# Down product of the last 1024 tokens with channels on partitions, by seven 2x2 products; weights kept, norm turned

## The chip, the cores and the metric

One core of a Trainium2 chip runs the program. The metric is the time of one execution on the device in microseconds (us), the median of several runs. Besides it there is one profiled execution, whose trace names every instruction of the five engines: PE (matmuls, and PEld for its weight loads), DVE, ACT, POOL, and SP, which here issues the transfers.

## The reference, cut to what matters

```python
mod = (silu(c) @ w_mod).reshape(1, 6, 1, -1)
sa, ca, ga, sb, cb, gb = (mod[:, i] for i in range(6))
h = layernorm(x) * (1 + ca) + sa
x = x + ga * A(h, k, v, ...)            # short and long causal convolution, gated
h = layernorm(x) * (1 + cb) + sb
x = x + gb * ((silu(h @ w_gate) * (h @ w_up)) @ w_down)
```
There are 2048 tokens of 512 channels; the hidden layer has 1792 channels. All is float32. The change concerns the last two lines.

## The kernel before, in words

The first part of the program (convolution through transforms) is not touched. After it the tokens lie in four tiles `xt[0]` to `xt[3]`, each with 128 tokens on the partitions, 4 rows and 512 channels. Tiles 0 and 1 are the first 1024 tokens (`q == 0`), tiles 2 and 3 the second 1024 (`q == 1`).

The feed-forward part goes over blocks `n` from 2 to 27 (`for n in range(G, 2 * NF)`, blocks 0 and 1 are done ahead of it): `f = n % 14` is a block of 128 hidden channels, `q = n // 14` the half of the tokens. So block 14 is the first of the second half and block 27 the last.

**Gate and up** of a block (`gate_up`) are one 2x2 product of matrices of blocks: gate and up against two halves of the 512 channels, and these against two sets of 512 tokens (`t` 0 and 1). It is done by seven products instead of eight (a Strassen-Winograd scheme). The operands of the weights are A11, A12, A22 (tile `wa`) and the sums S1 to S4 (tile `wsum`, made in `sr`); those of the tokens are B11, B21, B22 and the sums T1 to T4 (tiles `op` and `spare`, from the normed tokens `hraw`). Every operand is split into a high half (a cast on ACT to fp32r) and a low half (a subtraction on DVE or POOL); `seventh` is two channel blocks times the three passes of `PASSES`, six matmuls of 128x512. The seven products go into four PSUM tiles: `a` takes numbers 1 and 2, `b` 5 and 3, `c` 7 and 4, `d` 6. `p1` and `p5` are ACT's copies of a and b; DVE adds c to p5 and d to p1, and from these come gate and up for each t, SiLU on ACT, the product on DVE, and high and low halves of the activations `acts`. What belongs to t = 0 is finished in the next block (`late`, `finish`).

**Down** (`down`) is done for groups of G = 2 blocks, 256 hidden channels: for each t and each of 4 rows, six matmuls with the activations as the stationary operand and the down weights (`WD`, tile `wd`, multiplied by gb) moving; DVE adds the result `dn` to `xt`. Eight such products per group are handed out as fillers between the seven products (`downs`), four per block: one behind product 7, one behind 3, two behind 6. The last eight stand alone at the end, each followed by its store.

**Order.** Every instruction is kept in the order in which the program's text issues it on its engine (`InOrder`). Within a block the functions `behind(k)` run what the table `AT` and the loop put behind product k: splitting of the next block's weights (`split_w`, POOL and ACT), their loads, the norm of the second half, and the seven-product operands of the second half. PSUM has eight banks of 512; a tile gets a bank again once its reader is done.

**The norm of the second half**: `norm_stats`, then `norm2b` (tokens times rstd plus shift, on ACT and DVE), then `half_t` (transposes on PE, scale and bias on ACT into `hraw`), in blocks 4 to 8.

Of the kernel before, what the change touches and what calls it, by code (L numbers as in the profile page):

```python
# [10 lines left out]
F32 = mybir.dt.float32  # L11
F32R = mybir.dt.float32r
# [4 lines left out]
P = 128  # L17
# [38 lines left out]
def adaln_h3_swiglu(ctx, tc, q, kT, vT, shk, ssm, dskip, wgu, wdn, c, wmod, e_fwd, e_inv, w_c, out):  # L56
# [9 lines left out]
    def b16(name, shape=(P, 32, P), dt=F32):  # L66
# [3 lines left out]
        "401235670135260172635162432634623634642623634642652376243652376243"  # L70
    )

    def e8(shape, dt, name):
        return wp.tile(shape, dt, tag=f"e8_{next(homes8)}", name=name, bufs=1)
# [447 lines left out]
    def half_t(t, h):  # L522

        n, dst = nrm[t, h], raw_h[0][:, t % 2]
        pts = [p_.rearrange("p (b x) -> p b x", b=2) for p_ in two("nt")]
        for b in range(NB):
            for k in range(2):
                pe.transpose(pts[b // 2][:, b % 2, k * P : (k + 1) * P], n[:, k, b * P : (b + 1) * P], ident)
        for b in range(NB):
            act.activation(  # L530
                dst[:, b, 2 * h * P : 2 * h * P + 2 * P], pts[b // 2][:, b % 2], AF.Identity,
                scale=modT[:, 1, b : b + 1], bias=modT[:, 0, b : b + 1],
            )

# [43 lines left out]
    def split_w(f):  # L585
# [11 lines left out]
        s = e8([P, 2, 4, 2, P], F32R, "wsum")  # L597
# [6 lines left out]
        o = AOP[f] = {n: w[:, :, i] for i, n in enumerate(("A11", "A12", "A22"))}  # L604
        o.update({n: s[:, :, i] for i, n in enumerate(("S1", "S2", "S3", "S4"))})
# [14 lines left out]
    def wd_hi(g):  # L620
        wt = WD[g] = e8([P, 2, G, D], F32R, "wd")
        act.copy(wt[:, 0], stage["d", g])
# [5 lines left out]
    def split_wd(g):  # L628
        wd_mul(g)
        wd_hi(g)  # L630
        wd_lo(g)

# [34 lines left out]
    def downs(n):  # L667
        for _ in range(min(n, len(todo))):
            down(*todo.pop(0))

# [36 lines left out]
    def finish():  # L707

        if late:
            h, c_ = late.pop()  # L710
            act.copy(h[:, 0], c_)
            dve.tensor_tensor(h[:, 1], c_, h[:, 0].bitcast(F32), op=ALU.subtract)

    def gate_up(q, f, at={}):
# [5 lines left out]

        a = one("a")
# [3 lines left out]
        behind(1)  # L725
        b = one("b")
# [4 lines left out]
        behind(5)  # L731
        c_ = one("c")
# [3 lines left out]
        downs(1)  # L736
        seventh(a, f, 2, True)
        sg1 = g2("sg1")
        act.activation(sg1, a, AF.Silu)
        behind(2)  # L740
        seventh(b, f, 3, True)
        behind(3)
        downs(1)
        d = one("d")
        seventh(d, f, 6)
        dve.tensor_tensor(p1, p1, d, op=ALU.add)
        sg2 = g2("sg2")
        dve.tensor_tensor(sg2, p1, b, op=ALU.add)
        act.activation(sg2, sg2, AF.Silu)
        dve.tensor_tensor(d, p5, p1, op=ALU.add)  # L750
        behind(6)
        downs(2)
        dve.tensor_tensor(d, sg2, d, op=ALU.mult)
        h2 = acts[q, f, 1] = slots.pop(0)
        act.copy(h2[:, 0], d)
        seventh(c_, f, 4, True)
        dve.tensor_tensor(h2[:, 1], d, h2[:, 0].bitcast(F32), op=ALU.subtract)
        dve.tensor_tensor(c_, p1, c_, op=ALU.add)
        dve.tensor_tensor(c_, sg1, c_, op=ALU.mult)
        h1 = acts[q, f, 0] = slots.pop(0)  # L760
        late.append((h1, c_))
        behind(4)


    csil = cp.tile([P, 4], F32, name="csil")
    csb = cp.tile([P, 4, 32], F32, name="csb")
# [36 lines left out]
    wc = cp.tile([P, 384], F32, name="wc")  # L803
# [576 lines left out]
    def release(n):  # L1380
# [9 lines left out]
        (4, 7): lambda: norm_stats(2, range(0, 2)),  # L1390
        (4, 6): lambda: norm_stats(2, range(2, 4)),
        (5, 7): lambda: norm2b(2, 0),
        (5, 3): lambda: half_t(2, 0),
        (6, 7): lambda: norm2b(2, 1),
        (6, 3): lambda: half_t(2, 1),
        (6, 2): lambda: norm_stats(3, range(0, 2)),
# [91 lines left out]
```

## Time and profile before

| what | us |
|---|---|
| median of 3 runs | 598.99 |
| the runs | 598.84, 598.99, 601.92 |
| the profiled execution, first to last instruction (span) | 598.0 |
| PE busy | 583.2 |
| DVE busy | 457.0 |
| POOL busy | 329.9 |
| ACT busy | 302.7 |

The profiled execution's own time is given by its span; the runs' median is 1.0 above it. In rows of the timeline the columns are start, duration, engine, line, operation, output<-inputs, shapes and count, and in brackets the idle time before with what ended it. In grouped rows there stand total, mean in ns, and idle time before. Nearly every instruction has line 40, the helper that records it, so the tiles' names tell them apart.

### The profile page before, as it was taken

Reading aid. Unit: us, or ns where it says so; the run is one execution under the profiler, and the core shown is the slowest. Engines: PE = TensorE matmul, PEld = TensorE weight load, DVE = VectorE, ACT = ScalarE, POOL = GpSimd, SP = SyncE. Lnnn points to the kernel's source line nnn. Section 1 sums busy time; section 2 is a strip of 40 time slices with the busy share of each in tenths; the row PEclk is TensorE's granted clock in tenths of the full one; section 3 lists DMA queues with packets and bytes.
Section 4 is the critical chain, followed back from the end, with each engine's and each line's share of the span. In section 5 each row is a group of like instructions: output and inputs, shape, how many; then the busy total and the mean of one; then the engine's idle time right before and its main releaser. Section 6 shows DMA issues by size and latency. Waiting matters only on the chain.

```text
span 598.0 us, 10148 instructions
## 1 busy us (share of the span) xinstructions
PE 583.2 (98%) x4132; PEld 455.0 (76%) x4132; DVE 457.0 (76%) x585; ACT 302.7 (51%) x443; POOL 329.9 (55%) x264
## 2 busy tenths in 40 slices
PE   5999999999999999999999999999999999999997
PEld 4955756535988888888888888788888888888875
DVE  6999989978968878787778868975656565656555
ACT  1897989953574454445544435443434343434320
POOL 0003269692395896757467765766747474747200
PEclk7999999999999999999999999999999999999999
DMA  8998999999011021212120201243212110210003
GB/s 289 412 392 308 227 340 299 210 332 172 33 41 65 21 92 35 71 36 71 36 71 35 71 36 36 71 144 103 71 36 70 36 70 37 70 36 0 1 1 140
DMA packets 35423, 69.00 MB, mean 115 GB/s; under 512 B 2481, under 2 KB 18993, under 8 KB 33074
## 3 DMA queue, kind: packets, MB, share of 16 engines
q1 hardware_dynamic: 35378, 68.37, 37.0%
q8 instruction: 32, 0.52, 0.4%
q14 instruction: 13, 0.11, 0.1%
HBM read 55.78 MB, written 12.58 MB: 114 GB/s over the span
## 4 chain that ended last, share of the span: by engine, by line
PE 85%; DMA 6%; ACT 3%; DVE 2%; SPq 2%; issue 2%; ACTq 0%; DVEq 0%
PE dn L40 25%; PE a L40 12%; PE b L40 11%; PE c L40 11%; PE d L40 6%; PE s L40 5%; PE g L40 3%; DMA X<-away 2%; PE iv L40 2%; PE y L40 2%; PE px L40 2%; PE pk L40 2%; SPq L40 2%; DMA away<-X 2%; PE kt L40 1%
## 5 line engine op out<-in xcount | busy, mean ns | idle before, releaser
L40 PE MATMUL dn<-wd,acts 128*128 128x512 f32 x672 | 166.4, 391 | 0.5 <-DVE acts L40 0.4
L40 PEld LDWEIGHTS dn<-wd,acts 128*128 128x128 f32 x672 | 125.7, 188 | 27.6 <-DVE acts L40 1.1
L40 POOL TENSOR_TENSOR wa<-ws,wa 128x512 fp32r<-128x512 f32 (+1 forms) x52 | 61.7, 1209 | 111.8 <-ACT wa L40 104.0
L40 DVE TENSOR_TENSOR x<-x,dn 128x512 f32<-128x512 f32 x112 | 74.9, 681 | 50.6 <-PE dn L40 49.4
L40 PE MATMUL b<-op,wsum 128*128 128x512 f32 x312 | 79.2, 389 | 0.0
L40 POOL TENSOR_TENSOR wsum<-sr,wsum 128x1024 fp32r<-128x1024 f32 x26 | 71.4, 2745 | 0.0
L40 PEld LDWEIGHTS b<-op,wsum 128*128 128x128 f32 x312 | 58.5, 188 | 12.2
L40 ACT ACTIVATE sg<-sg 128x512 f32<-128x512 f32 x26 | 16.5, 633 | 85.4 <-DVE sg L40 85.4
L40 PE MATMUL a<-op,wa 128*128 128x512 f32 x228 | 57.9, 389 | 0.0
L40 PEld LDWEIGHTS a<-op,wa 128*128 128x128 f32 x228 | 42.8, 188 | 8.9
L40 DVE STREAM_TRANSPOSE X<-X 128x1024 f32<-128x1024 f32 x20 | 46.2, 2338 | 1.1 <-ACT X L40 1.1
L40 ACT CAST acts<-d 128x512 fp32r<-128x512 f32 x26 | 15.3, 587 | 62.5 <-DVE d L40 38.1
L40 POOL TENSOR_TENSOR vt<-u,vt 128x512 f32<-128x512 f32 x8 | 10.1, 1303 | 64.9 <-DMA x<-in_q 50.8
L40 POOL TENSOR_TENSOR s<-s,bcs 128x1024 f32<-128x1024 f32 x16 | 38.8, 2449 | 9.5 <-ACT s L40 9.3
L40 POOL TENSOR_TENSOR sr<-ws 128x256 f32<-128x256 f32 x52 | 43.5, 837 | 0.0
L40 POOL TENSOR_TENSOR wd<-wds,wd 128x1024 fp32r<-128x1024 f32 x14 | 35.4, 2529 | 9.6 <-ACT wd L40 9.6
L40 PE MATMUL c<-op,wa 128*128 128x512 f32 x156 | 39.7, 390 | 0.0
L40 PE MATMUL d<-op,wsum 128*128 128x512 f32 x156 | 39.6, 389 | 0.0
L40 PE MATMUL c<-op,wsum 128*128 128x512 f32 x156 | 39.6, 389 | 0.0
L40 DVE TENSOR_TENSOR acts<-c,acts 128x512 fp32r<-128x512 f32 x26 | 18.0, 692 | 21.5 <-ACT acts L40 21.5
L40 PEld LDWEIGHTS c<-op,wa 128*128 128x128 f32 x156 | 29.2, 188 | 6.3 <-DVE op L40 0.3
L40 PEld LDWEIGHTS d<-op,wsum 128*128 128x128 f32 x156 | 29.3, 188 | 6.1
(109 smaller groups left out, 1089.0 us busy)
## 6 DMA issues: line engine op xcount, KB each, us to landing
ws<-in_wgu SPq DMA_DIRECT2D x28, 512.0 KB, 3.2
wds<-in_wdn SPq DMA_DIRECT2D x14, 512.0 KB, 3.3
wm<-in_wmod SPq DMA_DIRECT2D x6, 1024.0 KB, 13.7
away<-X SPq DMA_DIRECT2D x3, 2048.0 KB, 10.4
X<-away SPq DMA_DIRECT2D x12, 512.0 KB, 11.2
x<-in_q SPq DMA_DIRECT2D x4, 1024.0 KB, 12.8
out<-x SPq DMA_DIRECT2D x16, 256.0 KB, 2.1
kt<-in_kT SPq DMA_DIRECT2D x3, 1024.0 KB, 7.1
```

Source lines behind the costliest of these rows:

```text
L40: return lambda *a, **k: self.tc.keep_in_program_order(f(*a, **k))
```

## The change

1. **Down products of groups 0 to 5 of the second half** are seven products of 2x2 blocks: two blocks of hidden channels and two halves of the output channels, against two sets of 512 tokens. Channels now lie on the partitions of the result. `sum_wd` makes the weights' sums (POOL), `pairs_wd` their high and low halves (`wda`, `wdt`). The activations' seven operands are made by `first_of` (B11, T1, behind block f even) and `second_of` (T2, T3, B22, then B21 and T4). `part_down` is one product for 128 output channels: three matmuls into a tile `dq`. Products 2, 3 and 4 are added to the residual `XT2` at once, products 1, 5, 7 and 6 to accumulators `acc`, which `fold` adds up and into XT2 in blocks 26 and 27. Group 6 is done plainly by `down_t`, weights stationary, with stores into a second output of channels by tokens.
2. **Fillers** in the second half: ten parts in an even block, four in an odd one behind product 1 (`PARTS`); in blocks 14 and 15 the plain down products of the first half. In the second half the order of the products in a block is 1, 5, 7, 6, 3, 2, 4 where it was 1, 5, 7, 2, 3, 6, 4.
3. **The norm** of the second half: mean and deviation go through memory and come back spread over all partitions (`spread`), the tokens are transposed raw (`turn`, kept as XT2), multiplied on POOL and added to on DVE (`times_rs`, `plus_rs`), then scaled on ACT.
4. **Prepared gate and up weights** of blocks 2 to 13 are written to memory in the first half (`keep_w`) and read back in the second (`fetch_w`), where before they were loaded and prepared again.

The first place is PE in block 14. Before, its rows from a's first product to c's second; d<-op,wsum is product 6, a<-op,wa product 2, c<-op,wa product 4 (A22 with T4):

```order
L40 MATMUL a<-spare,wa 128x512 x6
L40 MATMUL b<-op,wsum 128x512 x6
L40 MATMUL c<-op,wsum 128x512 x6
L40 MATMUL dn<-wd,acts 128x512 x6
L40 MATMUL a<-op,wa 128x512 x6
L40 MATMUL b<-op,wsum 128x512 x6
L40 MATMUL dn<-wd,acts 128x512 x6
L40 MATMUL d<-op,wsum 128x512 x6
L40 MATMUL dn<-wd,acts 128x512 x12
L40 MATMUL c<-op,wa 128x512 x6
```
The same block in the changed kernel:

```order
L40 MATMUL a<-spare,wa 128x512 x6
L40 MATMUL b<-op,wsum 128x512 x6
L40 MATMUL c<-op,wsum 128x512 x6
L40 MATMUL dn<-wd,acts 128x512 x6
L40 MATMUL d<-op,wsum 128x512 x6
L40 MATMUL dn<-wd,acts 128x512 x12
L40 MATMUL b<-op,wsum 128x512 x6
L40 MATMUL dn<-wd,acts 128x512 x6
L40 MATMUL a<-op,wa 128x512 x6
L40 MATMUL c<-op,wa 128x512 x6
```
a's second product moved from fifth to ninth place, directly ahead of c's second.

The second place is ACT in the same block, where op<-hraw is the high half of T4 and sg<-a the SiLU of a's second product. Before:

```order
L40 CAST wa<-ws 128x256
L40 CAST wsum<-sr 128x1024
L40 ACTIVATE sg_3748<-a 128x512
L40 CAST op<-hraw 128x1024
L40 ACTIVATE sg_3777<-sg_3777 128x512
L40 CAST acts<-d 128x512
```
And now:

```order
L40 CAST wsum<-sr 128x1024
L40 ACTIVATE b_3832<-b_3832 128x512
L40 ACTIVATE sg_3788<-a 128x512
L40 CAST op<-hraw 128x1024
L40 COPY p_3868<-a 128x512
```
The cast of T4 kept its place behind the SiLU of a, and the other SiLU (of t = 1) moved ahead of both.

The third place is DVE in block 27, from c's sum for p5 to the last low half. Before:

```order
L40 TENSOR_TENSOR p_5206<-p_5206,c 128x512
L40 TENSOR_TENSOR x_542<-x_542,dn 128x512 x2
L40 TENSOR_TENSOR p_5197<-p_5197,d 128x512
L40 TENSOR_TENSOR sg_5256<-p_5197,b 128x512
L40 TENSOR_TENSOR d<-p_5206,p_5197 128x512
L40 TENSOR_TENSOR x_542<-x_542,dn 128x512 x2
L40 TENSOR_TENSOR d<-sg_5256,d 128x512
L40 TENSOR_TENSOR acts<-d,acts 128x512
```
And now, where xt is XT2, and the rows of 1024 with acc are the folds:

```order
L40 TENSOR_TENSOR xt_2623<-xt_2623,acc 128x1024
L40 TENSOR_TENSOR xt_2909<-xt_2909,dq 128x512 x2
L40 TENSOR_TENSOR xt_2909<-xt_2909,acc 128x1024 x2
L40 TENSOR_TENSOR xt_2623<-xt_2623,dq 128x512 x4
L40 TENSOR_TENSOR acts_3860<-c,acts_3860 128x512
L40 TENSOR_TENSOR wds<-wds,bcs 128x1024
L40 TENSOR_TENSOR p_5326<-p_5326,c 128x512
L40 TENSOR_TENSOR p_5294<-p_5294,d 128x512
L40 TENSOR_TENSOR sg_5360<-p_5294,b 128x512
L40 TENSOR_TENSOR d<-p_5326,p_5294 128x512
L40 TENSOR_TENSOR d<-sg_5360,d 128x512
L40 TENSOR_TENSOR acts_3860<-d,acts_3860 128x512
```
Ahead of p5's sum there now stand three folds, six adds of parts, and the multiply of the last group's down weights.

The diff, cut to its core:

```diff
+    def spread(t):
+        w = dp.tile([2, TB, P], F32, tag=f"rs{t}", name=f"rs{t}")
+        sp.dma_start(w.rearrange("k i p -> p k i"), to[f"b{t}"])
+        RS[t] = r4([P, 2, 512], F32, f"rs{t}")
+        sp.dma_start(RS[t], w.rearrange("k i p -> k (i p)")[None].to_broadcast([P, 2, 512]))
...
+    def keep_w(f):
+        w, s = WS[f]
...
+            sp.dma_start(m, t.bitcast(F32))
...
+    def sum_wd(g):
+        st = stage["d", g]
+        pool.tensor_tensor(st, st, bcs[:, None, 2, :].to_broadcast([P, G, D]), op=ALU.mult)
+        a11, a21, a12, a22 = (st[:, k, h * H : h * H + H] for k in range(2) for h in range(2))
+        t = r4([P, 4, H], F32, "wdr")
...
+    ORDER = (1, 5, 7, 6, 3, 2, 4)
+    def part_down(g, n, k):
+        o = one("dq")
+        a, b = ROP[g][PROD[n][0]], LOP[g][PROD[n][1]]
+        for i, (wa, xa) in enumerate(PASSES):
+            pe.matmul(o, a[:, wa, k * P : (k + 1) * P], b[:, xa], start=(i == 0), stop=(i == 2))
+        if n in INTO:
+            t, b0 = INTO[n]
+            xv = XT2[2 + t][:, b0 + k]
+            dve.tensor_tensor(xv, xv, o, op=ALU.add)
+            return
...
+        if g:
+            dve.tensor_tensor(ACC[n][:, k], ACC[n][:, k], o, op=ALU.add)
+        else:
+            act.copy(ACC[n][:, k], o)
...
+    def fold(k):
+        c11, c21, c12, c22 = (XT2[2 + t][:, h : h + 2] for t in range(2) for h in (0, 2))
+        for e, o, i in (
+            ((dve, c11, ACC[1]), (pool, ACC[6], ACC[1])),
+            ((dve, c12, ACC[5]), (dve, c22, ACC[5]), (pool, ACC[7], ACC[6])),
+            ((pool, c12, ACC[6]), (pool, c21, ACC[7])),
+            ((pool, c22, ACC[7]),),
+        )[k]:
+            e.tensor_tensor(o, o, i, op=ALU.add)
...
+    def second_of(f, t, raw):
+        o = LOP[f // G]
+        if t:
+            t3, t2 = RAW["B12"], RAW["T1"]
+            dve.tensor_tensor(t3, raw, t3, op=ALU.subtract)
+            dve.tensor_tensor(t2, raw, t2, op=ALU.subtract)
+            for n, r, e in (("T3", t3, dve), ("T2", t2, pool), ("B22", raw, pool)):
+                o[n] = slots.pop(0)
+                hi_lo(o[n], r, e)
+            return
...
+        def first():
+            seventh(a, f, 2, True)
+            act.activation(sg1, a, AF.Silu)
+            behind(2)
+            fill("a2")
...
+        if q:
+            first()
         seventh(c_, f, 4, True)
...
+    PARTS = ({"c1": 2, "d": 2, "b2": 2, "a2": 2, "c2": 2}, {"a1": 4})
...
+            if m % G == 0:
+                at[3].append(lambda: load_wd(g1))
+                if g1 < NG - 1:
+                    at[6].append(lambda: sum_wd(g1))
+                else:
+                    at[4].append(lambda: fold(0))
+            elif g1 < NG - 1:
+                at[7].append(lambda: pairs_wd(g1))
+            else:
+                at[1].append(lambda: fold(1))
+                at[5].append(lambda: split_wd(g1, 6))
+                at[7].append(lambda: fold(2))
+                at[3].append(lambda: fold(3))
...
-    downs(8)
+    for t in (1, 0):
+        for b in range(NB):
+            down_t(NG - 1, t, b)
```
In the table `AT` the entry `(14, 2): lambda: then("T4", "B21")`, the split of T4, is the same in both kernels.

More of the change, by code (lines that the diff above doesn't have):

```diff
@@ L596, in split_w @@
         pool.tensor_tensor(sr[:, 3], a12, sr[:, 1], op=ALU.subtract)
-        s = e8([P, 2, 4, 2, P], F32R, "wsum")
+        s = e8([P, 2, 4, 2, P], F32R, "wsum", home)
         act.copy(s[:, 0], sr)
@@ new lines, in down_t @@
+    def down_t(g, t, b):
+        o = one("dn")
+        for fl in range(G):
+            for n, (wa, xa) in enumerate(PASSES):
+                pe.matmul(
+                    o, WD[g][:, wa, fl, b * P : (b + 1) * P], acts[1, g * G + fl, t][:, xa],
+                    start=(fl == n == 0), stop=(fl == G - 1 and n == 2),
+                )
+        xv = XT2[2 + t][:, b]
+        dve.tensor_tensor(xv, xv, o, op=ALU.add)
+        sp.dma_start(out_t[b * P : (b + 1) * P, t].rearrange("d i p -> d (i p)"), xv)
```

266 lines of the change are left out of this document (199 added, 67 removed).

## The prediction, made before the changed kernel was run

> **What bounds the kernel now.** I read the page first, then the list of waits of the tensor engine, then a table by stretches, then the timeline of single blocks. The fences stand in this order.
>
> ```profile
> span 598.0 us, 10148 instructions
> PE 583.2 (98%) x4132; PEld 455.0 (76%) x4132; DVE 457.0 (76%) x585; ACT 302.7 (51%) x443; POOL 329.9 (55%) x264
> ```
> ```profile
> PE s L40 <- DMA er<-in_e_fwd: 5.8, 1, 5.8
> PE dn L40 <- DVE acts L40: 0.4, 2, 0.2
> ```
> ```profile
> 387.00:582.00 195.00, 195.00 (x862) 161.50 (x861) 123.76 (x181) 73.35 (x121) 107.89 (x89) 1.00 0.15 53
> ```
> ```profile
> 554.64 1.52 PE L40 MATMUL c<-op,wsum 128*128 128x512 f32 x6
> 556.00 1.52 PE L40 MATMUL dn<-wd,acts 128*128 128x512 f32 x6
> ```
> PE is the bound: from 387 to 582 us it is never idle, at a granted clock of 1.00, and in the whole feed-forward stage it waits 0.4 us, for activations at two places. So what counts there is the number of matmuls times their spacing, plus every wait that the new order lets in. Six matmuls start 1.36 us after the six before them, 0.227 us each; I call this 1.36 us a product. The span is 598.0; the runs' median is 598.99, so about 1.0 lies around the span and I sum against 599.0.
>
> **What is saved.** In six groups the down product takes 7 products of 2 channel blocks of 3 passes, 42 matmuls, where 8 products of 6 took 48. That is 36 matmuls, 36 x 0.227 = 8.2 us off the bound, if PE stays as full as it is. The turned norm leaves PE its 32 transposes, merely bunched; the weights kept in memory cost PE nothing. Everything else is a question of waits, at three places.
>
> **Place one: T4 in block 14.** These rows are the same work in the kernel before: ACT reads a's second product (SiLU), then casts T4's high half, DVE makes its low half, and c's second product needs both.
>
> ```profile
> 377.70 1.53 PE L40 MATMUL a<-op,wa 128*128 128x512 f32 x6
> 378.32 1.22 DVE L40 TENSOR_TENSOR op<-hraw,op 128x1024 fp32r<-128x1024 f32 x1
> 380.71 0.59 ACT L40 ACTIVATE sg<-a 128x512 f32<-128x512 f32 x1
> 382.05 1.05 ACT L40 CAST op<-hraw 128x1024 fp32r<-128x1024 f32 x1 [0.74 <-DVE hraw L40]
> 382.57 2.40 POOL L40 TENSOR_TENSOR wsum<-sr,wsum 128x1024 fp32r<-128x1024 f32 x1
> 383.13 2.92 DVE L40 TENSOR_TENSOR op<-hraw,op 128x1024 fp32r<-128x1024 f32 x1 [0.52 <-ACT op L40]
> 385.87 1.66 PE L40 MATMUL c<-op,wa 128*128 128x512 f32 x6
> 386.10 0.99 PEld L40 LDWEIGHTS c<-op,wa 128*128 128x128 f32 x5 [0.27 <-DVE op L40]
> ```
> Before, five products lay between a's second product (377.70) and c's (385.87), and the low half still came 0.27 late. The change puts a's second product directly ahead of c's, and the split of T4 still hangs behind it, so nothing covers it. From the end of a's product c waits: about 0.2 for the result, SiLU 0.59, cast 1.05, hops 0.1, low half 1.22 when free, less the 0.23 of the one matmul that needs the high half alone: 2.9 us. The dear end: ACT has the other SiLU still to do (0.7 more; its input now waits behind one more add), and the low half takes 2.92 as in the row instead of 1.22: 5.3. POOL's new multiply of the down weights falls into this stretch, but need not hit it; I take 4.4, nearer the row of the same operation.
>
> **What DVE's operations cost.** DVE operations with one operand in PSUM take 0.69 and follow each other by 0.60, or by 0.72 where one needs the other. Those with both inputs in SBUF are another matter:
>
> ```profile
> 428.37 0.69 DVE L40 TENSOR_TENSOR p<-p,d 128x512 f32<-128x512 f32 x1 [0.67 <-PE d L40]
> 429.09 0.69 DVE L40 TENSOR_TENSOR sg<-p,b 128x512 f32<-128x512 f32 x1
> 429.69 1.15 DVE L40 TENSOR_TENSOR d<-p,p 128x512 f32<-128x512 f32 x1
> 444.65 0.69 DVE L40 TENSOR_TENSOR d<-p,p 128x512 f32<-128x512 f32 x1
> ```
> ```profile
> 365.08 2.39 POOL L40 TENSOR_TENSOR wsum<-sr,wsum 128x1024 fp32r<-128x1024 f32 x1
> 370.93 2.40 POOL L40 TENSOR_TENSOR wd<-wds,wd 128x1024 fp32r<-128x1024 f32 x1 [3.46 <-ACT wd L40]
> ```
> ```profile
> 365.15 3.40 DVE L40 TENSOR_TENSOR op<-hraw,op 128x1024 fp32r<-128x1024 f32 x1 [1.29 <-ACT op L40]
> 371.52 2.36 DVE L40 TENSOR_TENSOR d<-p,p 128x512 f32<-128x512 f32 x1
> ```
> ```profile
> L40 DVE TENSOR_TENSOR d<-p,p 128x512 f32<-128x512 f32 x26 | 30.8, 1184 | 0.0
> L40 DVE TENSOR_TENSOR wds<-wds,bcs 128x1024 f32<-128x1024 f32 x13 | 18.4, 1417 | 0.0
> L40 POOL TENSOR_TENSOR wa<-ws,wa 128x512 fp32r<-128x512 f32 x25 | 33.9, 1357 | 105.3 <-ACT wa L40 97.6 <-PE dn L40 7.7
> L40 POOL TENSOR_TENSOR sr<-ws 128x256 f32<-128x256 f32 x50 | 41.1, 822 | 0.0
> L40 ACT COPY p<-a 128x512 f32<-128x512 f32 x26 | 15.3, 590 | 13.1 <-PE a L40 13.1
> ```
> d<-p,p takes 0.69 alone, but 2.36 when it starts 0.6 after a POOL operation of 2.40: it stands until POOL is done (373.33) and then runs. The same holds at 365.15. The mean over 26 is 1.18, so a meeting costs 0.5 on average and up to 2.4. Per pair of blocks the old kernel had two such DVE operations of 512 and one of 1024; the new one has ten of 512 (sums, SiLU times up, T1 to T4, two low halves), while POOL stays about as busy. It was busy 107.89 of 195 us, 55%; now it no longer prepares gate and up weights, but has per pair five low halves of activations (1.36 each), three of down weights (2.4, 1.36 and half of that), the multiply (about 2.4) and four sums (0.82 each): 17.0 of 28.6, 59%.
>
> **Place two: the seam of odd and even blocks.** A pair is now 126 matmuls, 28.6 us, where it was 132, 29.9. DVE has 24 operations with a PSUM operand (24 x 0.62 = 14.9) and ten others (6.9 free, 11.8 at the mean): 21.8 to 26.7 us, so it doesn't bind on average. But behind the odd block they come in a row. From b's second product in the odd block (2.5 us before the even block begins) DVE does gate sum 0.7, five both-SBUF operations, two on c, two more for T4 and B21's low half, p5+c and the add of the first part, 8.2 free, and is done at 5.7. That first part's bank is given to the fifth part, which PE reaches at 9.5. POOL is then at two down-weight low halves (2.4 and 1.36) and two of activations (1.36 each), and meeting all of them costs about 4.2: done at 9.9, 0.4 late. Bounds: 0, if half the meetings miss, and 1.0, if the waits on ACT's casts (0.59 each) add to it. Six even blocks: 0 to 6, taken 2.4.
>
> **Place three: the end.** Here is the end before, in the timeline of PE:
>
> ```profile
> 581.85 1.36 PE L40 MATMUL dn<-wd,acts 128*128 128x512 f32 x4
> 583.43 10.31 PE L40 MATMUL dn<-wd,acts 128*128 128x512 f32 x44 [0.22 <-DVE acts L40]
> ```
> PE waited 0.22 there. Now, in block 27, DVE's queue holds three folds of 1024 and the multiply of the last down weights ahead of p5+c, and the last products need three things at its far end: c's second product needs p5+c, the first down product needs POOL's low half of those weights, its fourth matmul the activations' high and its fifth the low half. DVE, from the seventh part's add in block 26: 16 operations with a PSUM operand (9.9), four of 1024 with both inputs in SBUF (5.3; 1.42 is the mean of the multiply, 1.22 the free one), one of 512 (0.69), one stop for ACT (0.7): 16.6. Counted from the start of block 26, that begins at 13.3 and ends at about 30, where PE as the order has it needs the high half at 29.2: with two small bank waits, 1.2 late. But POOL does two accumulator sums back to back just when the first folds come, and the low half of the weights when d<-p,p comes: 1.2, 1.35 and 1.7 of waiting by the start times this gives, 4.2 in all, so 5.4; and if the seam's backlog (3 us) is still there, 8.4. On the way the bank waits show: d waits for the add of the first part of block 27, which stands behind the folds. I take 6.5. The last store is as before.
>
> By the mean row a meeting is worth 0.5, and the three would come to 1.5 and the end to 2.7 without, 5.7 with the backlog. The Trainium skill ("SBUF — State Buffer", section "Who interferes with whom") says that a DVE instruction with two SBUF inputs fully blocks against a GpSimd operation that reads SBUF until the first is done. By that rule the three cost their whole remainders; the row at 365.15 (1.08 of work behind a wait for 367.47) agrees with the rule, the mean only averages hits and misses.
>
> **What is hidden.** In the first half, blocks 4 to 8, POOL gets four multiplies of 1024 and DVE four adds; POOL stood idle 4.2 us a block ahead of wa's low half (105.3 over 25), and the results are wanted at block 9, so I count nothing; a missed cover would cost up to 1 us. The kept weights:
>
> ```profile
> ws<-in_wgu SPq DMA_DIRECT2D x28, 512.0 KB, 3.2
> away<-X SPq DMA_DIRECT2D x3, 2048.0 KB, 10.4
> ```
> One block's prepared weights are 768 + 1024 KB. By these rows they land in 9 to 11 us; the request waits for c's second product of the block before, and there are at least 13.6 us until use, so nothing again. On SP the two tiny norm transfers stand ahead of a weight load that has a block of slack.
>
> **The sum.** -8.2 + 4.4 + 2.4 + 6.5 = +5.1 on 599.0: 604.
>
> **Rivals.** First, *the saving comes through*: the meetings of DVE and POOL at the seam and the end miss each other. The point that decides is which of the two starts first; at the seam it is 0.35 us between POOL's 1024 low half and DVE's p5+p1. For it: 444.65 ran free, 0.69. Against: the mean of 1.18, and over three times as many tries. Then -8.2 + 2.9 + 0 + 1.2 = -4.1: 595. Second, *half of it*: T4 2.9, seam 0.5, end 4.4: 598.6. Third, *DVE becomes the bound*: each both-SBUF operation meets POOL, the backlog isn't worked off, and each pair loses 1.0: 3.6 more, 608. Against it the 26.7 of 28.6 us. Fourth, *the clock falls* after T4's wait. The rows of the kernel's start, by stretches (the third number from the end is the granted clock):
>
> ```profile
> 5.00:10.00 5.00, 0.13 (x1) 0.00 (x0) 3.94 (x4) 0.20 (x1) 0.00 (x0) 0.86 1.03 381
> 12.00:14.00 2.00, 2.00 (x20) 1.78 (x20) 2.00 (x3) 0.99 (x2) 0.00 (x0) 0.50 1.09 392
> 16.00:18.00 2.00, 1.39 (x14) 1.26 (x11) 2.00 (x5) 0.10 (x1) 0.00 (x0) 1.00 1.08 433
> ```
> After PE's wait of 5.8 us the clock is 0.50 for about 4 us of work: 2 us lost. My wait of 4.4 is shorter and broken by one matmul, so by this row alone it need not fall; if it does, 606. The Trainium skill ("TensorE: Matmul & The Clock Gate", Part 1) puts the idle window that halves the clock at about 3.4 us; by that rule T4's wait would do it, and the trace of before has no wait of this length to say. Fifth, the kept weights land late: at 15 us instead of 11, some 1.4 in each of 12 blocks, 17 more, above 615; the free transfer engines (share 0.15) speak against it.
>
> **How the numbers follow.** Forecast 0.46, own range 600 to 608; saving comes through 0.15; half of it 0.14; DVE bound 0.13; clock 0.08; weights late 0.04. About 0.5%, 3 us, is what a measurement can tell from no change, so "same" is 596 to 602. Faster: 0.12 of the first rival. Same: its other 0.03, 0.14, and 0.08 of the forecast's lower part, 0.25. Slower: 0.38 + 0.13 + 0.08 + 0.04 = 0.63. The range of 8 in 10 leaves out the faster end and the late weights: 596.5 to 609.5.
>
> **What would show it.** In the new profile: 3072 matmuls in the program's order with PE's list of waits holding one of 3 to 5 us on c for op in block 14 (right), or none (place one wrong); PE waits of about 0.4 at dq for an acc add in even blocks; d, c and dn in the last block waiting for DVE and POOL, together 5 to 8. If the dq waits are near 0 and the last block's under 2, the meetings miss and the first rival holds; a time under 596 makes the prediction wrong, as does a wait on the kept weights.

## The result, and the profile after

The changed kernel takes 623.28 us (median of 4 runs, 618.61 to 626.74), the kernel before 600.45 in the runs beside it: a ratio of 1.0375, 95% interval 1.0315 to 1.0435. Slower was forecast, at 604; it is 23 us slower and not 5. The runs of the changed kernel lie 8 us apart, so sizes of a few us are taken from the traces below, between the same instructions of one kernel and the other. A run that fell into a slower state of the chip is left out of medians and ratios here and below; that was one run of e10 (624.16 us).

The page of the changed kernel, span and busy times:

```profile
span 618.9 us, 10224 instructions
PE 586.6 (95%) x4096; PEld 451.4 (73%) x4096; DVE 500.4 (81%) x622; ACT 297.6 (48%) x441; POOL 350.2 (57%) x261
```
PE has 36 matmuls fewer and is no longer full: 95% where it was 98%. From its list of waits (total, times, longest); of these rows the kernel before had only the first:

```profile
PE s L40 <- DMA er<-in_e_fwd: 5.1, 1, 5.1
PE dn L40 <- ACT acts L40: 3.8, 3, 2.6
PE b L40 <- POOL wsum L40: 3.6, 3, 1.9
PE c L40 <- DVE op L40: 2.1, 1, 2.1
PE c L40 <- ACT op L40: 2.1, 1, 2.1
PE a L40 <- ACT p L40: 1.7, 1, 1.7
PE dn L40 <- ACT xt L40: 1.6, 1, 1.6
PE d L40 <- DVE xt L40: 1.5, 1, 1.5
...
PE dn L40 <- POOL wd L40: 1.3, 1, 1.3
PE b L40 <- DVE xt L40: 1.2, 1, 1.2
```
Two of them are place one (c for op), three are place three (d and b for xt, dn for wd). The others, for wsum, for ACT's copies p and xt and most of those for acts, were in no step of the prediction: they lie in blocks 5 to 10, in the first half. PE's first products of block 4 and of block 11 bound that stretch. In the kernel before:

```profile
218.09 1.52 PE L40 MATMUL a<-op,wa 128*128 128x512 f32 x6
326.67 1.52 PE L40 MATMUL a<-op,wa 128*128 128x512 f32 x6
```
And in the changed kernel:

```profile
220.88 1.29 PE L40 MATMUL a<-op,wa 128*128 128x512 f32 x5
344.42 1.52 PE L40 MATMUL a<-op,wa 128*128 128x512 f32 x6
```
108.6 us before, 123.5 now: 15.0 of the 20.9 us between the two spans are lost in blocks 4 to 10, where the down product isn't touched at all. Of the 15.0, PE's waits make 10.5; more than half of the rest is PE at a lower granted clock behind them, 0.92 over block 6 (255.12 to 277.15), where it is busy about 2.5 us longer than in e5 and e8, which have 1.00 there. The rest of the 20.9 by the same reading: the start of the program 2.8 (PE does the same there before and after; in the runs below block 4 begins anywhere between 216.8 and 222.5, so this is scatter), block 14 +4.5, block 15 +1.0, blocks 16 to 26 -5.1, block 27 to the end +2.7.

What stands first in blocks 4 to 7, on SP and on the two engines that split the weights (start, duration, and in brackets the wait ahead):

```profile
231.94 0.37 SPq L40 DMA_DIRECT2D rs<-rsb  x1
243.95 0.32 SPq L40 DMA_DIRECT2D rs<-rs  x1
244.36 0.38 SPq L40 DMA_DIRECT2D ws<-in_wgu  x1
244.80 0.42 SPq L40 DMA_DIRECT2D kept<-wa  x1
...
246.61 0.93 SPq L40 DMA_DIRECT2D ws<-in_wgu  x1
```
```profile
rs<-rsb SPq DMA_DIRECT2D x2, 4.0 KB, 11.2
```
```profile
250.86 0.74 POOL L40 TENSOR_TENSOR sr<-ws 128x256 f32<-128x256 f32 x1 [11.32 <-DMA ws<-in_wgu]
```
```profile
252.64 0.93 ACT L40 CAST wa<-ws 128x512 fp32r<-128x512 f32 x2 [6.18 <-DMA kept<-wa]
```
The norm's store, 4 KB in 1024 pieces of 4 bytes, takes 11 us until it has landed. The load back needs it, so SP stands from 232 to 244, and behind it stand the next weight load, the stores of the kept weights and the weight load after that. POOL then waits 11.32 us for the first, ACT 6.18 us for a kept store that must have read the tile wa before the cast may overwrite it.

### The profile page after: what moved, and what is told of

The parts are those of the page before. It is cut to its first block, busy times and chain, and to the rows that moved or that the text cites. A ratio compares the mean times of both kernels' runs of the same rounds, so it can differ in the third digit from the quotient of the medians.

```text
span 618.9 us, 10224 instructions
## 1 busy us (share of the span) xinstructions
PE 586.6 (95%) x4096; PEld 451.4 (73%) x4096; DVE 500.4 (81%) x622; ACT 297.6 (48%) x441; POOL 350.2 (57%) x261
## 4 chain that ended last, share of the span: by engine, by line
PE 75%; DVE 15%; ACT 4%; DMA 3%; issue 2%; POOL 1%; SPq 0%; DVEq 0%; ACTq 0%; POOLq 0%
PE dn L40 10%; PE b L40 9%; PE a L40 8%; PE c L40 8%; PE dq L40 8%; PE s L40 5%; PE d L40 5%; PE iv L40 4%; PE px L40 3%; PE pk L40 3%; PE g L40 3%; PE y L40 2%; DVE d L40 2%; PE kt L40 2%; DMA wds<-in_wdn 2%
## 5 line engine op out<-in xcount | busy, mean ns | idle before, releaser
L40 PE MATMUL dn<-wd,acts 128*128 128x512 f32 x336 | 84.8, 394 | 4.6 <-ACT acts L40 2.8
L40 PEld LDWEIGHTS dn<-wd,acts 128*128 128x128 f32 x336 | 63.1, 189 | 19.3 <-ACT acts L40 3.7
L40 POOL TENSOR_TENSOR wa<-ws,wa 128x512 fp32r<-128x512 f32 (+1 forms) x28 | 38.4, 1393 | 41.9 <-ACT wa L40 41.9
L40 DVE TENSOR_TENSOR x<-x,dn 128x512 f32<-128x512 f32 x56 | 37.1, 679 | 14.9 <-PE dn L40 14.6
L40 POOL TENSOR_TENSOR s<-s,bcs 128x1024 f32<-128x1024 f32 x16 | 38.8, 2444 | 10.5 <-ACT s L40 10.3
L40 POOL TENSOR_TENSOR acts<-sg,acts 128x512 fp32r<-128x512 f32 x12 | 15.6, 1298 | 41.8 <-ACT acts L40 41.8
L40 PE MATMUL dq<-acts,wdt 128*128 128x512 f32 x144 | 36.9, 391 | 0.0
L40 POOL TENSOR_TENSOR sr<-ws 128x256 f32<-128x256 f32 x28 | 28.4, 1014 | 11.6 <-DMA ws<-in_wgu 11.6
L40 POOL TENSOR_TENSOR wsum<-sr,wsum 128x1024 fp32r<-128x1024 f32 x14 | 34.5, 2464 | 0.5 <-ACT wsum L40 0.5
L40 DVE TENSOR_TENSOR xs<-pk,xs 128x1024 f32<-128x1024 f32 x24 | 28.3, 1217 | 7.1 <-PE pk L40 5.3
L40 PEld LDWEIGHTS c<-op,wsum 128*128 128x128 f32 x156 | 29.2, 188 | 6.5 <-DVE x L40 0.5
```

The lines of the kernel that those rows point to most:

```text
L40: return lambda *a, **k: self.tc.keep_in_program_order(f(*a, **k))
```

## The experiments

Theory one: SP's queue, held by the norm's store. Rival two: the stores of the kept weights by themselves. Rival three: the turned norm's own work and order on POOL, DVE and ACT. All runs in one table; the third column is the stretch of blocks 4 to 10 between the two rows shown above, in each kernel's trace. Each kernel has one trace, of one of its runs.

| run | median us, ratio to before (95%) | blocks 4 to 10 |
|---|---|---|
| before | 599.2 to 601.2 in the six sets of runs beside the others | 108.6 |
| changed | 623.28, 1.0375 (1.0315 to 1.0435) | 123.5 |
| e1 norm behind the load | 619.88, 1.0308 (1.0224 to 1.0392) | 125.1 |
| e2 before, with the norm's trip | 604.45, 1.0068 (1.0033 to 1.0103) | 112.7 |
| e3 before, with kept stores | 599.66, 0.9966 (0.9939 to 0.9993) | 108.7 |
| e4 T4 early | 616.26, 1.0223 (1.0151 to 1.0295) | 123.8 |
| e5 store in rows | 617.22, 1.0278 (1.0231 to 1.0325) | 119.4 |
| e6 before, with trip and kept stores | 613.67, 1.0228 (1.0171 to 1.0284) | 123.7 |
| e7 end folds later | 614.08, 1.0230 (1.0169 to 1.0290) | 122.2 |
| e8 e4, e5 and e7 together | 608.44, 1.0109 (1.0044 to 1.0174) | 117.8 |
| e9 e8 and the norm's order | 598.48, 0.9971 (0.9948 to 0.9994) | 112.6 |
| e10 the norm's order alone | 615.10, 1.0246 (1.0206 to 1.0287) | 122.9 |
| e11 e9 with the 4-byte store | 612.75, 1.0208 (1.0180 to 1.0237) | 124.3 |
| e12 e9, folds between the adds | 598.86, 0.9975 (0.9954 to 0.9995) | 113.7 |
| e13 e9, folds in store order | 599.27, 0.9974 (0.9945 to 1.0003) | 112.5 |
| e14 e9 with T4 late | 605.51, 1.0069 (1.0043 to 1.0094) | 112.4 |
| e15 e9 with the end as changed | 603.44, 1.0037 (1.0009 to 1.0064) | 112.6 |

Kernels that are the same up to block 10 show how far the third column can be trusted: 122.2 to 123.8 (changed, e4, e7), 117.8 and 119.4 (e8, e5), 112.4 to 113.7 (e9, e12 to e15). So it scatters by up to 1.6 us.

### The first half: e1, e2, e3, e6

**e1** moves the two trips behind the weight loads:

```diff
-        (4, 7): lambda: spread(2),
-        (6, 1): lambda: spread(3),
...
             at[7].append(lambda nf=(n + 2) % NF: load_w(nf))
+        if n in (4, 6):
+            at[7].append(lambda t=n // 2 if n == 4 else 3: spread(t))
```


> The changed kernel with one thing moved: the two norm transfers of each tile (spread) stand on SP behind the next gate and up weight load instead of ahead of it, for tile 3 in block 6 after that block's load instead of behind its first product. Theory one (SP's order: the norm store waits for POOL's deviation, its 4 KB take about 11 us to land, SP waits for that before it issues the load back, and the weight load behind it comes 15 us late): of the about 15 us by which blocks 4 to 10 were longer, 10 to 14 go; 609 to 613 us, the tensor engine's waits for wsum under 1 us. Rival two (the stores of the kept weights load the transfer engines and hold buffers) and rival three (the turned norm's own work on POOL, DVE and ACT): nothing of either is touched, 620 to 626 us as the changed kernel, waits as there.

**e2** adds the trip to the kernel before, **e3** adds the kept stores:

```diff
+        RSX[t] = ffn["s"].tile([P, 512], F32, tag="rsx", name=f"rs{t}")
+        sp.dma_start(RSX[t], w.rearrange("k i p -> k (i p)")[0:1].to_broadcast([P, 512]))
...
+        (4, 7): lambda: spread(2),
+        (6, 1): lambda: spread(3),
```
```diff
+        if n < NF:
+            at[2].append(lambda f=f: keep_w(f))
```


> The kernel before, with the norm's trip through memory added at the changed kernel's places on SP (statistics as early as there; the load back brings half as much, 256 KB, and nobody reads it; the norm itself stays the old one). Theory one: the weight loads of blocks 6 and 8 are issued some 12 to 15 us late and PE waits for wsum: 606 to 613 us. Rivals two and three: no kept weights and no new norm work, so 599 to 602 as the kernel before.

> The kernel before, with the prepared weights of blocks 2 to 13 also written to memory (keep_w at the changed kernel's places; nobody reads them back). Rival two: the first half is longer by 8 to 15 us, 608 to 615. Theory one: SP has slack for them and the transfer engines too, at most 2 us: 599 to 603. Rival three: as the kernel before.

Theory one fell in the form in which it was put: in e1 the weight load is no longer behind the store, and the stretch is no shorter, 125.1 where it was 123.5. Kept stores alone cost nothing (108.7), the trip alone 4.1, between what the two theories expected. What e1 has in the load's stead, on SP and ACT:

```profile
229.60 0.37 SPq L40 DMA_DIRECT2D rs<-rsb  x1
240.30 0.32 SPq L40 DMA_DIRECT2D rs<-rs  x1
240.66 0.43 SPq L40 DMA_DIRECT2D kept<-wa  x1
```
```profile
246.61 0.93 ACT L40 CAST wa<-ws 128x512 fp32r<-128x512 f32 x2 [2.47 <-DMA kept<-wa]
257.02 1.05 ACT L40 CAST wd<-wds 128x1024 fp32r<-128x1024 f32 x1 [6.36 <-DMA kept<-wsum]
```
The weights come in time, but their cast waits for the kept store, which now stands behind the norm's store; so does the cast of the down weights, whose tile reuses the place of an earlier wsum. The theory that remained: whatever stands behind the slow store is late, and the kept stores make that a wait on ACT. **e6** puts both into the kernel before, with its old norm and old down product (the edits of e2 and e3 together).

> The kernel before with both additions, the norm's trip through memory (604.5 alone) and the kept weights' stores (599.7 alone); nobody reads either, the old norm and the old down product stay. If the loss is the two together on SP's queue (the kept stores stand behind the norm's store, and hold the buffers of wa and wsum until they have run): clearly more than the sum of the two, 608 to 615. If the two only add: 603 to 605, and the rest of the first half's loss is the turned norm's own work (rival three).

15.1 us, as much as the changed kernel loses there and more than three times 4.1 + 0.1, with none of the turned norm's work. That the two sizes are equal is partly chance, since the changed kernel has a second cause, as e5 shows below. Nor is all of it waiting: PE stands 8.6 us, against 3.3 in e2, and behind the two long waits the granted clock falls, to 0.86 over block 5 (232.87 to 256.79) and 0.84 over block 6 (256.79 to 279.07), where PE is busy 6.3 us longer than before; in e2 the clock stays at 1.00. The waits are the same in kind, first ACT's, then PE's:

```profile
247.48 0.93 ACT L40 CAST wa<-ws 128x512 fp32r<-128x512 f32 x2 [8.10 <-DMA kept<-wa]
...
262.02 1.04 ACT L40 CAST wd<-wds 128x1024 fp32r<-128x1024 f32 x1 [8.73 <-DMA kept<-wsum]
```
```profile
251.51 2.93 PE L40 MATMUL dn<-wd,acts 128*128 128x512 f32 x6 [3.55 <-ACT sg L40]
265.05 1.95 PE L40 MATMUL dn<-wd,acts 128*128 128x512 f32 x3 [3.17 <-ACT acts L40]
```
ACT's queue is in order: behind the waiting cast stand the SiLU and the activations' cast, and PE's down products wait for those, not for weights.

### The store's shape and the norm's order: e5, e10, e9, e11

**e5** turns the 128x8 values on PE and stores 8 rows of 512 bytes; both trips stand between two weight loads:

```diff
-        sp.dma_start(w.rearrange("k i p -> p k i"), to[f"b{t}"])
+        pt = one("rt")
+        pe.transpose(pt[0:8, 0:P], to[f"b{t}"].rearrange("p k i -> p (k i)"), ident)
+        r = RS[t][0:8, 0, 0:P]
+        act.copy(r, pt[0:8, 0:P])
+        sp.dma_start(w.rearrange("k i p -> (k i) p"), r)
...
-        (4, 7): lambda: spread(2),
-        (5, 1): lambda: norm_stats(3, range(0, 2)),
+        (5, 1): lambda: (norm_stats(3, range(0, 2)), spread(2)),
-        (6, 1): lambda: spread(3),
-        (6, 5): lambda: plus_rs(2, 0),
+        (6, 5): lambda: (spread(3), plus_rs(2, 0)),
```


> The changed kernel with the norm's store made of 8 rows of 512 bytes (one small transpose on PE, a copy on ACT, then the store) instead of 1024 pieces of 4 bytes, and both tiles' trips put behind the weight load of the block and ahead of the next. The kept weights and the turned norm's own work stay. Theory one, as the run with the trip behind the load left it (SP stands about 11 us until the store has landed, and whatever stands behind it is late: a weight load, or a store of kept weights that holds a buffer which ACT's cast needs): the store lands in about 2 us, and 9 to 12 of the 15 us in blocks 4 to 10 go: 611 to 614. Rival two (the kept stores by themselves): excluded by the kernel before with kept stores, 599.7. Rival three (the turned norm's work on POOL, DVE and ACT): the 15 us stay, 619 to 625.

SP's queue now waits 0.9 us per store (the list of its waits in e5: total, times, longest):

```profile
SPq L40 <- DMA rs<-rs: 1.9, 2, 0.9
```
But only 4.1 us of the 15 went: block 6 is 6.9 shorter, but block 7 2.8 longer. What took their place is a second cause, rival three, in block 7; here ACT's rows and PE's wait:

```profile
272.22 1.52 ACT L40 ACTIVATE hraw<-hraw,modT 128x512 f32<-128x512 f32 x2 [3.22 <-DVE hraw L40]
273.64 0.56 ACT L40 COPY p<-a 128x512 f32<-128x512 f32 x1
...
275.06 2.06 ACT L40 COPY xt<-nt 128x512 f32<-128x512 f32 x4
```
```profile
275.72 2.65 PE L40 MATMUL dn<-wd,acts 128*128 128x512 f32 x6 [3.56 <-ACT xt L40]
```
The scaling of the norm's last part waits for DVE's add and stands ahead of the copies of a and b, and those ahead of the copies that free the transposes' banks. **e10** moves just these two steps in the changed kernel; **e9** does so in e8 (e4, e5 and e7 together) and moves POOL's deviation of tile 2 behind the next weights' split:

```diff
-        (6, 4): lambda: plus_rs(2, 1),
-        (8, 4): lambda: plus_rs(3, 1),
+        (7, 5): lambda: plus_rs(2, 1),
+        (9, 5): lambda: plus_rs(3, 1),
```
```diff
-        (4, 5): lambda: norm_stats(2, range(2, 4)),
+        (4, 6): lambda: norm_stats(2, range(2, 4)),
```


> The changed kernel with only the two last shifts (plus_rs) moved behind the copies of a and b of blocks 7 and 9; the store of 4-byte pieces, T4 and the end stay. By the store theory the loss of blocks 5 to 7 is SP's and stays (622 less the 1.7 to 2 of block 9): 618 to 622. If the norm's order makes the larger part of the 15 us: 613 to 617.

> The changed kernel with three of these edits together: T4 early, the norm's store in rows, the folds later. If the three losses are separate, they add: 623.3 less 7.0 (measured for T4), less 9 to 12, less 4 to 5, so 599 to 603, and the saving of the down products shows only then. If a loss moves elsewhere when another goes (DVE or POOL full), 606 or more.

> The run with three changes (608.4), and the norm's own work put in another order: the second statistics of tile 2 behind product 6 of block 4, so that POOL's deviation stands behind the split of the next weights and no longer ahead of it; the last shifts of both tiles (plus_rs, and the ACT scaling that waits for them) behind block 7's and block 9's copies of a and b instead of ahead of them. In the run with the store in rows, blocks 4 to 10 were still 10.9 us longer than before, with PE waits in block 5 (0.56 and 1.26 for POOL), block 7 (3.56 for ACT's xt copies) and block 9 (1.67 for ACT's p copy). If the norm's order makes these (rival three, for the part that the store did not make), 7 to 10 us go and all four waits with them: 599 to 602 as a median, the span under 595 at a full clock, that is level with the kernel before or up to 1% under it. If POOL and DVE are simply too full there, the waits move on and 605 or more stays.

e10's median, 615.1, lies where the norm's order was to make the larger part. Its trace, of a run of 619.2, says otherwise: the stretch is 122.9, 0.6 less than in the changed kernel. Block 7's and block 9's waits are gone (4.6 us), but block 10 has a new one of 2.25 us for acts and is 3.4 longer, with a granted clock of 0.91 over it, and block 6 is 0.6 longer at 0.85. What the runs of 614 to 615 gained isn't shown. e8 came out at 608.4, in its second expectation, though the run that was traced took 602.7; the store was not the only cause in blocks 4 to 10, block 7's and block 9's waits are in it as in e5. From e8 to e9, with the store out of the way, the order and the deviation's place are worth 5.3 (117.8 to 112.6): blocks 4 and 5, where two waits for POOL go, 1.7, blocks 7 and 9 4.7, and block 10 takes 1.2 back. So there are two causes, and what one edit gives depends on the other: the store alone taken away gives 4.1, the order alone 0.6, both with the deviation's place 11.0. The deviation's place was not tried by itself. **e11** turns only e9's store back, at the same place on SP:

> The run with all edits, and only the norm's store turned back into 1024 pieces of 4 bytes, at the same place on SP behind the first product of blocks 5 and 6. If SP's stand of about 11 us is what costs, it holds up block 7's weight load and the kept stores again: 6 to 12 us above the run with all edits. If behind the load there is slack for it once the norm's order is right: under 2 us above it.

11.7 us in the stretch, 14.3 in the median. One row each of ACT and PE carries most of it; most of the rest is a granted clock of 0.81 over block 6 (253.24 to 280.24):

```profile
264.52 1.04 ACT L40 CAST wd<-wds 128x1024 fp32r<-128x1024 f32 x1 [18.47 <-DMA kept<-wsum]
```
```profile
267.55 1.94 PE L40 MATMUL dn<-wd,acts 128*128 128x512 f32 x3 [9.38 <-ACT acts L40]
```

### T4 and the end: e4, e7, e14, e15, e12, e13

**e4** splits T4 as soon as it is made, **e14** undoes that in e9:

```diff
-        (14, 7): lambda: diff("B21", "B21", "B11"),
-        (14, 2): lambda: then("T4", "B21"),
+        (14, 7): lambda: (diff("B21", "B21", "B11"), then("T4", "B21")),
```


> The changed kernel with T4's high half (ACT) and low half (DVE) issued behind product 7 of block 14, directly after their difference, and no longer behind a's second product. If place one is what the trace shows, the two waits of c for op in block 14 (2.10 and 2.11 us) go, and with them the clock of 0.95 in block 15 (1.0 us): 4 to 5.5 us under the changed kernel, about 618. Rival: ACT and DVE are full there, so that the split delays p5's sum or the activations and the wait only changes its tile: 0 to 2 us under it, a new wait of 2 to 4 us in blocks 14 or 15.

> The run with all edits (598.5), and only T4's split put back behind a's second product. If place one costs what the trace of the changed kernel shows, two waits of 2.1 us and 1 to 2 us of lower clock behind them: 604 to 606. If the median's 7.0 us of the run with T4 early was the whole truth: 605.5 as well, but if most of it was scatter, 602 to 603.5.

Both waits of c go in e4, blocks 14 and 15 take 14.96 each where they took 20.35 and 15.96, and no new wait comes. Undone in e9 they take 20.77 and 15.35, 6.2 more; the ratio to before goes from 0.9971 to 1.0069, 0.0098 x 600 = 5.9. Place one with what hangs on it is about 6.

**e7** hands DVE's folds and the last down weights out anew, **e15** undoes that in e9:

```diff
-            ((dve, c11, ACC[1]), (pool, ACC[6], ACC[1])),
-            ((dve, c12, ACC[5]), (dve, c22, ACC[5]), (pool, ACC[7], ACC[6])),
+            ((pool, ACC[6], ACC[1]),),
+            ((pool, ACC[7], ACC[6]),),
...
+            ((dve, c22, ACC[5]), (dve, c11, ACC[1]), (dve, c12, ACC[5])),
...
-                at[1].append(lambda: fold(1))
-                at[5].append(lambda: split_wd(g1, 6))
+                at[1].append(lambda: split_wd(g1, 6))
+                at[1].append(lambda: fold(1))
...
     finish()
+    fold(4)
```


> The changed kernel with the end put in another order: DVE's three folds stand behind the last activations' low half, and the last down weights are multiplied and split behind the last block's first product instead of its second. If place three is what the trace shows (folds ahead of the adds that free PE's banks, the weights' multiply behind them), PE's tail waits (1.15, 1.45, 1.30, 1.01, 0.22 = 5.1 us) shrink to 1 or less: 4 to 5 us under the changed kernel, 618 to 619.5. Rival: the folds then stand ahead of the last adds and stores and the end comes late all the same, under 2 us gained.

> The run with all edits (598.5), and only the end put back: DVE's folds and the last down weights' multiply at the changed kernel's places. By the trace the tail waits of 5.1 us come back and the 2.4 us behind the last matmul go: 600.5 to 602.5. If the 9.2 us of the run with the end alone were real: 606 to 608.

The tail waits are gone in e7 but for 0.23. Of e7's 9.2 us in the median its trace shows 3.2 from block 27 to the end (30.6 where it was 33.8); the rest of what its trace gains lies ahead of the edit, mostly in the start (3.0) and blocks 4 to 10 (1.3), and is scatter. Undone in e9 the end costs 0.0066 x 600 = 4.0 net. **e12** and **e13** tried for the 2.4 us that e9 now loses behind its last matmul, by placing each of DVE's folds directly ahead of two of the last adds. In e12 one fold stands behind the stores it should have reached, so the stored values of tile 3's first two channel blocks lack accumulator 5; e13 has it in the right place.

> The run with all edits (598.5), and the last folds handed out: POOL folds the two halves of tile 3 first, and DVE's three folds stand each directly ahead of the two last adds that follow it, instead of all three ahead of the eight adds. In the run with all edits PE was done at 588.4 and the span ended 6.7 us later, where it was 4.3 in the kernel before; DVE waited 2.08 us for POOL's folds with the eight adds behind it. If that is what held the end, 2 to 2.5 us go: 596 to 596.8, about 0.6% under the kernel before. If the stores behind the adds set the end, under 0.5 us goes.

> The run with all edits (598.5), with POOL's last three folds in the order in which the last products are added (tile 3's first half, its second half, then tile 2's second half), and each of DVE's three folds directly ahead of the two adds to the same half. DVE need not wait for POOL's last fold then. If the folds' place holds the end: the span ends 4.3 to 5 us behind PE's last matmul instead of 6.7, 1.7 to 2.4 us gained, 596 to 597. If the stores hold it: under 0.5 us gained.

Neither gained. In e12 the first adds still wait 2.09 us for POOL. In e13 DVE's first fold no longer waits for a result, but stands until POOL's folds are done (575.57 + 7.58 = 583.15):

```profile
575.57 7.58 POOL L40 TENSOR_TENSOR xt<-xt,acc 128x1024 f32<-128x1024 f32 x3
```
```profile
580.99 3.23 DVE L40 TENSOR_TENSOR xt<-xt,acc 128x1024 f32<-128x1024 f32 x1
```
It is the meeting of the prediction, in its plainest form: 3.23 instead of 1.22. With the folds split between DVE and POOL the end stays there; that no better order exists wasn't shown.

e9 is the version to keep: 598.48, a ratio of 0.9971 (0.9948 to 0.9994), about 0.3% under the kernel before. The saving of the down products is whole in it; blocks 4 to 10 take back 4.0 us, the end 2.5.

## Why the prediction was wrong

**The step that failed** is "What is hidden", which put the first half at nothing. It cost 15.0 us, and two of its sentences share them. The larger one is the last: "On SP the two tiny norm transfers stand ahead of a weight load that has a block of slack". In e11 this store alone costs 11.7. The other is that the turned norm's work on POOL and DVE is covered, "so I count nothing; a missed cover would cost up to 1 us": a better order and another place for the deviation were worth 5.3 (e8 to e9), and 4.0 of the stretch are still lost in e9. On SP I looked at what stands behind the trip in the change as a weight load with slack. What I left out is the duration of the store, for which the trace of before had no row of the kind (its store rows are of 256 to 2048 KB), and I bounded it from no side; that SP issues nothing while a load waits for a store; and that the kept stores, counted as hidden by free transfer engines, stand in the same queue and hold tiles that ACT's casts need. The kept stores were free by themselves (e3: 0.1), as I had counted them; the trip was not (e2: 4.1), and the two together cost 15.1 (e6). I also left out, in the first half, the lower clock behind PE's waits. The Trainium skill ("DMA: Bandwidth & Descriptors", section "Rules for kernel authors") says that a last dimension that isn't contiguous lowers to one descriptor per element and should be rearranged; the trace agrees that the shape matters, 11.2 us to landing for 1024 pieces of 4 bytes against a wait of 0.9 for 8 rows.

**What is saved**, 8.2: right. Blocks 16 to 26 took 164.55 us before and 159.46 now, block 27 has four parts of three matmuls where it had four products of six, 2.7 less; 5.1 + 2.7 = 7.8, and blocks 16 to 26 by the count of their matmuls would be 159.1.

**Place one**, 4.4: the wait was right, 2.10 + 2.11 = 4.2. First ACT and DVE, then PE:

```profile
404.08 1.04 ACT L40 CAST op<-hraw 128x1024 fp32r<-128x1024 f32 x1
```
```profile
405.14 2.57 DVE L40 TENSOR_TENSOR op<-hraw,op 128x1024 fp32r<-128x1024 f32 x1 [0.72 <-ACT op L40]
```
```profile
405.16 0.49 PE L40 MATMUL c<-op,wa 128*128 128x512 f32 x1 [2.10 <-ACT op L40]
407.77 2.08 PE L40 MATMUL c<-op,wa 128*128 128x512 f32 x5 [2.11 <-DVE op L40]
```
The other SiLU stood ahead, and the low half took 2.57, as at the dear end: it began 1.1 us behind POOL's new multiply of the down weights (404.02, 2.61) and ended 1.1 us behind its end. What was missing is the rival that I gave 0.08: the clock fell. By stretches, the third number from the end is the clock:

```profile
405.16:407.77 2.61, 0.49 (x1) 0.19 (x2) 2.56 (x1) 0.00 (x0) 2.53 (x2) 1.00 0.00 0
407.77:412.00 4.23, 4.23 (x12) 3.32 (x13) 2.04 (x3) 0.00 (x0) 2.64 (x4) 0.60 0.19 54
412.00:426.00 14.00, 14.00 (x63) 11.59 (x62) 6.24 (x11) 4.62 (x8) 6.86 (x5) 1.00 0.48 191
```
4.23 us at 0.60 is 1.7 lost: the two waits, parted by one matmul, act as one. Blocks 14 and 15 together are 5.5 longer. The fall is no chance of this trace: e1, e5, e7, e10 and e14 have the two waits and a clock of 0.50 behind them. I had argued from the one long wait at the start that a shorter, broken one need not do it.

**Place two**, 2.4: wrong, it was 0. The first pair of blocks takes 16.32 + 12.24 = 28.56, exactly 126 matmuls, the later ones up to 0.1 more, and there are no dq waits. The meetings came as predicted, only with room. Here in the seam of blocks 25 and 26, POOL's low half of the weights, DVE's rows and PE's fifth part:

```profile
566.48 2.39 POOL L40 TENSOR_TENSOR wdt<-wdr,wdt 128x1024 fp32r<-128x1024 f32 x1
```
```profile
566.78 2.64 DVE L40 TENSOR_TENSOR p<-p,p 128x512 f32<-128x512 f32 x1
...
577.40 1.27 DVE L40 TENSOR_TENSOR acc<-acc,dq 128x512 f32<-128x512 f32 x2
```
```profile
578.22 1.58 PE L40 MATMUL dq<-acts,wdt 128*128 128x512 f32 x6
```
I had the first part's add done at 9.9 us into the even block and the bank wanted at 9.5. The block begins at 568.70; the first of the two adds is done at about 578.0, 9.3, the bank wanted at 578.22, 9.5. I was 0.6 us off, more than the 0.4 that was to be the wait, and six times 0.4 was the whole term.

**Place three**, 6.5: right in kind, 5.4 in size, within its bounds. The meetings came where they were put, here the first fold (free 1.22) and POOL's accumulator sums:

```profile
586.34 5.72 POOL L40 TENSOR_TENSOR acc<-acc 128x1024 f32<-128x1024 f32 x2 [8.03 <-DVE acc L40]
```
```profile
587.57 2.24 DVE L40 TENSOR_TENSOR xt<-xt,acc 128x1024 f32<-128x1024 f32 x1
```
This fold lost 1.0, the other two together 0.8, and d<-p,p, 2.19 instead of 0.69 beside POOL's low half of the weights, 1.5: 3.3 where I had 4.2. (The four operations of 1024 come to 5.1 by the prices named there, not 5.3.) PE's rows in block 27 and behind it:

```profile
590.46 1.66 PE L40 MATMUL b<-op,wsum 128*128 128x512 f32 x6 [1.15 <-DVE xt L40]
...
594.93 1.66 PE L40 MATMUL d<-op,wsum 128*128 128x512 f32 x6 [1.45 <-DVE xt L40]
...
602.00 0.96 PE L40 MATMUL dn<-acts,wd 128*128 128x512 f32 x3 [1.30 <-POOL wd L40]
603.97 0.50 PE L40 MATMUL dn<-acts,wd 128*128 128x512 f32 x1 [1.01 <-ACT acts L40]
```
With the 0.22 behind them these are 5.1.

**The sum** as it came, from span to span: -7.8 + 5.5 (blocks 14 and 15) + 0 + 5.4 + 15.0 + 2.8 (the start) = 20.9. Without the first half and the start it would have been 3.1, under my 5.1 and at the edge of what I had called "same". The three places came out 1.1 above, 2.4 below and 1.1 below what I had for them. That the kernel came out clearly slower is the first half's doing, so my "slower" was right by luck. The fifth rival, over 615, came out in number but not in mechanism: the kept weights' loads of the second half make no wait; it is their stores in the first half that were late. DVE did not become the bound. (The 3072 matmuls named under "What would show it" stand in no row; the page has 4096, 36 fewer than before.)

## What to carry to other kernels

Before a transfer is called hidden, give it a duration by its pieces and not its bytes, and list what stands behind it on the issuing queue, with the tiles that those transfers hold. Two edits on one in-order queue can cost more than three times the sum of what each costs alone, and two losses in one stretch cover for each other: taking away one shows little, so test also the other way round, by putting one back into a kernel that has neither. Here a store of many 4-byte pieces was best turned on the chip first. A long wait of PE is to be counted with the lower clock that may come behind it.

## What the hardware did that I had not expected

- 4 KB in 1024 pieces took 9.0 to 14.4 us to land (medians of e2 and e6; 11.2 in the changed kernel), nearly as long as 2048 KB in the rows of before (10.4).
- A large store beside it was slow too. In e11 ACT waited until 264.52 for a kept store of wsum issued at 249.02, with the 4-byte store issued behind it at 251.78; in e9, without such a store, the like wait ended 9.7 us after the issue. Whether the pieces slow their neighbours was not tested by itself.
- Two PE waits of about 2 us with one matmul between them brought the clock down in all six traces that have them, in the changed kernel to 0.60 for 4.2 us. The Trainium skill ("TensorE: Matmul & The Clock Gate", Part 1) speaks of a free-running window of about 3.4 us; the trace fits that, 4.2 idle of 4.7 us, if a window with one matmul in it counts as idle, which the six traces suggest.
- A wait of the same length may or may not bring the clock down. Behind block 7's wait for xt the granted clock was 0.50 to 0.54 from 276 to 279 us in e5 (wait 3.56), and 1.00 throughout in e8 (wait 3.54), which makes 1.6 us between the two traces.
